# Fourteen weight-slice copies moved from VectorE to GpSimd, and five instead of eight plain-float32 tiles, in a fused attention and two-layer MLP kernel

## The chip, the cores and the metric

The kernel runs on one NeuronCore of a Trainium2 chip. The metric is the device time of one execution in microseconds. Engines are called as in the profile: PE is TensorE (matmul), PEld its weight loads, DVE is VectorE, ACT is ScalarE, POOL is GpSimd, SP issues the DMAs. A line number such as L405 is a line of the kernel before.

## The reference

Inputs are float32 (the weights arrive as 64-bit floats and are taken apart inside the kernel). First a linear recurrence per head over 768 steps, 4 batches, 8 heads, head size 48:

```
for t in range(S):
    cur   = u * k_t (outer) v_t
    y_t   = r_t @ (state + cur)
    state = w * state + k_t (outer) v_t
x = y, as 3072 rows of 384
h = x @ w_in              # 384 -> 2048, layer 1
g = h * tanh(softplus(h))
x = g @ w_out             # 2048 -> 384
h = relu(x @ w2_in)       # layer 2
out = (h * h) @ w2_out
```

## The kernel before, in words

The sequence is cut into 6 chunks of 128 steps. For each chunk the attention gives 512 columns of x (4 batches by 128 steps). `BLOCKS` lists 12 blocks of work, each one layer on one chunk; a block has 16 tiles, one for each slice of 128 of the 2048 hidden columns. Tile number i runs over all 192 tiles; tiles 0 to 15 are the first block, layer 1 on chunk 0. For each tile PE does an "up" product into a PSUM tile h (128x512), ACT and DVE apply the activation, and PE does a "down" product that is added into accumulators acc.

**Precision.** A float32 operand is written as the sum of a high part rounded to the shorter format fp32r and a low part (the rest, also fp32r). A product of two such pairs takes three fp32r matmuls (`mm3`, L809 to L812: high by high, high by low, low by high). So an up takes 9 matmuls, and a down of layer 1 too (3 column groups by 3). For tiles in the set `FULL` (L40) the down is done differently: `act1` does not split the activation g, and `down1` multiplies the unsplit g with the unsplit weight `WF[1, j]` in plain float32, 3 matmuls (L934), each of which the trace shows as two records. A tile in `FULL` therefore skips two DVE instructions in `halves`: the high part (L904) and the low part (L909). The product with h that comes before (L872) is done for both kinds.

**Weights.** `convert(layer, j, ...)` (L351 to L411) brings one slice of weights, 128x768, from 64-bit words to the pair of high and low part. For layer 1 the steps are: a DMA load `raw`; ACT L366 and L372; DVE L376 and L383, after which `f` (the ring "wf") is the float32 weight; the high part, `hi`; and on DVE L410 the low part, f minus hi. For slices 0 and 1 the high part is made by ACT (L407); for the other 14 (`j >= WHIGH`) by DVE (L405). The up of tile j in the first block needs hi and lo of slice j. The ring "wf" has 6 buffers, so slice j can't write f before the last reader of slice j-6 is done: the low part L410, or for a tile in `FULL` its plain-float32 down. Converted slices are stored to DRAM (`keep`) and loaded again for later blocks.

**Order.** The program is not written in the order in which it runs. Every step is given to `plan.add` with an engine, an assumed duration, a due time, and the tiles it reads and writes. `Plan.order` (L139) then plays a list schedule: at each moment each free engine takes, of the steps that are ready, the one with the earliest due time. The order that comes out is the order in which each engine's instructions are issued, and each engine works strictly in that order. A changed engine or duration of one step can so change the order of the others. Attention work for later chunks (`unit`) is spread among the tiles in the same way. The ScalarE functions of the first 32 tiles are done in groups (`GROUPS`): Tanh for each tile, then Arctan and Sin for a group, with a table load between.

POOL has very little work in this kernel: some memsets and four small copies (`pads`, L658), all in the first 14 us.

Of the kernel before, what the change touches and what calls it, by code (L numbers as in the profile page):

```python
# [36 lines left out]
TRIG = sum(GROUPS)  # L37
GROUP_OF = [(sum(GROUPS[:g]), n) for g, n in enumerate(GROUPS) for _ in range(n)]
HIGH, WHIGH = 32, 2
FULL = frozenset(range(0, 8))  # L40


class Tl:
# [67 lines left out]
class Plan:  # L111
# [8 lines left out]
    def add(self, eng, dur, due, fn, r=(), w=(), deps=(), late=0.0, table=""):  # L120

        it = dict(n=len(self.items), eng=eng, dur=dur, due=due, fn=fn, deps=list(deps), after=[], ready=0.0, late=late, table=table)
        for t in r:
            if t.writer:
                it["deps"].append(t.writer)
        for t in w:
            it["deps"] += t.readers
            if t.writer:
                it["deps"].append(t.writer)
        for t in r:  # L130
            t.readers.append(it)
            t.users.append(it)
        for t in w:
            t.writer, t.readers = it, []
            t.users.append(it)
        self.items.append(it)
        return it
# [67 lines left out]
def rwkv_moe_kernel(ctx: ExitStack, tc: tile.TileContext, good, rk, nat, wuT, wrow, ub, cst, w1, w2, out):  # L205
    nc = tc.nc
# [41 lines left out]
    def f32v(ap):  # L248
        return ap.bitcast(F32)
# [3 lines left out]
    add = plan.add  # L253

    def dma(o, i, eng=nc.sync):
        eng.dma_start(out=o, in_=i)
# [88 lines left out]
    def parts(layer, j, again=""):  # L345

        t = R[f"w{j}"].new([128, 2, 768], F32R, f"w{layer}_{j}{again}")
        W[layer, j] = [t.part(lambda ap, i=i: ap[:, i]) for i in range(2)]
        return t, *W[layer, j]

    def convert(layer, j, due, load_due):  # L351

        raw = R[f"w{j}"].new([128, 768, 2], U32, f"raw{layer}_{j}")
        t, hi, lo = parts(layer, j)
        f = WF[layer, j] = R["wf"].new([128, 768], F32, f"wf{layer}_{j}")
        src = (w1, w2)[layer - 1][j]

        def load():
            o = raw.get().rearrange("p (h d) t -> p h (d t)", h=2)
            dma(o, src.rearrange("h p d -> p h d").bitcast(U32))  # L360

        def fu():
            return f.get().bitcast(U32)

        def s0():
            nc.scalar.activation(f.get(), raw.get()[:, :, 1].bitcast(F32), AF.Copy, scale=HSC)  # L366

        on_act = layer == 1

        def s1():  # L370
            x = raw.get().rearrange("p d t -> p (d t)").bitcast(U8).rearrange("p (d t) -> p d t", t=8)[:, :, 3]
            nc.scalar.activation(raw.get()[:, :, 0].bitcast(I32), x, AF.Copy, scale=1 / 32, bias=-15.5 / 32)  # L372

        def s2():
            if on_act:
                nc.vector.scalar_tensor_tensor(  # L376
                    fu(), fu(), 3, raw.get()[:, :, 0], ALU.logical_shift_left, ALU.bitwise_or
                )
            else:
                nc.vector.tensor_scalar(fu(), fu(), 3, None, ALU.logical_shift_left)  # L380

        def s3():
            nc.vector.scalar_tensor_tensor(fu(), raw.get()[:, :, 1], 0x80000000, fu(), ALU.bitwise_and, ALU.bitwise_or)  # L383

        def s4():
            nc.vector.scalar_tensor_tensor(
                fu(), raw.get()[:, :, 0], 29, fu(), ALU.logical_shift_right, ALU.bitwise_or
            )

        it = add("SP", 0.786, load_due, load, w=[raw])  # L390
        if layer == 2:
            gates.append((it, int(load_due)))
        elif j >= 6:
            gates.append((it, -1))
        add("ACT", 0.9, due - 1.5, s0, r=[raw], w=[f])
        if on_act:
            add("ACT", 0.9, due - 1.3, s1, r=[raw], w=[raw])
            add("DVE", 0.96, due - 1, s2, r=[raw, f], w=[f])
            add("DVE", 0.96, due - 0.8, s3, r=[raw, f], w=[f])
        else:  # L400
            add("DVE", 0.55, due - 1, s2, r=[f], w=[f])
            add("DVE", 0.96, due - 0.8, s3, r=[raw, f], w=[f])
            add("DVE", 0.96, due - 0.6, s4, r=[raw, f], w=[f])
        if layer == 1 and j >= WHIGH:
            add("DVE", 0.56, due, lambda: nc.vector.tensor_copy(hi.get(), f.get()), r=[f], w=[hi])  # L405
        else:
            add("ACT", 0.87, due, lambda: nc.scalar.activation(hi.get(), f.get(), AF.Copy), r=[f], w=[hi])  # L407
        add(
            "DVE", 0.96, due + 0.5,
            lambda: nc.vector.tensor_tensor(lo.get(), f.get(), f32v(hi.get()), ALU.subtract), r=[f, hi], w=[lo],  # L410
        )  # L411
# [404 lines left out]
    def turn(i, extra=0.0):  # L816

        b = GROUP_OF[i][0] if i < TRIG else i
        return b + 0.02 * (i - b) + extra
# [18 lines left out]
    def act1(i, blk, h):  # L838

        e = R["e"].new([128, 512], F32, f"e{i}")  # L840
        full = i in FULL
        g = R["ghi"].new([128, 512], F32, f"g{i}") if full else e
        d = i + 1
        if i < TRIG:
# [6 lines left out]
            if i + 1 == sum(GROUP_OF[i]):  # L851
# [17 lines left out]
                for n, x, o, p in now:  # L869
# [3 lines left out]
                    )  # L873
                    late.append((n, o, None) if n in FULL else (n, *halves(n, o, turn(n, 2.2))))
            return late
# [21 lines left out]
    def halves(i, g, due, square=None):  # L897
        hi = R["ghi"].new([128, 512], F32R, f"ghi{i}")
        lo = R["glo"].new([128, 512], F32R, f"glo{i}")
        if square:  # L900
            add("ACT", 0.63, due, lambda: nc.scalar.activation(hi.get(), square.ap, AF.Square), r=[square], w=[hi])  # L901
        else:
            if i < HIGH:
                add("DVE", 0.42, due, lambda: nc.vector.tensor_copy(hi.get(), g.ap), r=[g], w=[hi])  # L904
            else:
                add("ACT", 0.63, due, lambda: nc.scalar.activation(hi.get(), g.ap, AF.Copy), r=[g], w=[hi])  # L906
        add(
            "DVE", 0.69, due + 0.2,
            lambda: nc.vector.tensor_tensor(lo.get(), g.ap, f32v(hi.ap), ALU.subtract), r=[g, hi], w=[lo],  # L909
        )  # L910
        return hi, lo
# [89 lines left out]
    for j in range(NF):  # L1001
        convert(1, j, j - 1, -140 + j)
# [21 lines left out]
    for i in range(NS):  # L1024
# [22 lines left out]
        if blk == 0:  # L1047
            keep(1, j, NF + j)
        elif blk + 1 < len(BLOCKS) and BLOCKS[blk + 1][0] != layer:
            if layer == 2:  # L1050
                again(1, j, i + LAG + 1)
            elif (2, j) in kept:
                again(2, j, i + LAG + 1)
            else:
                convert(2, j, i + LAG + 4 + 0.3 * j, i + LAG)
                keep(2, j, i + LAG + 14)
# [258 lines left out]
```

## Time and profile before

| | |
|---|---|
| runs (us) | 913.98, 917.95, 919.26; median 917.95 |
| profiled execution (us) | 914.35 |
| its span (us) | 912.6 |
| PE busy | 900.1 us (99%), 5225 instructions |
| DVE busy | 549.9 us (60%) |
| ACT busy | 581.1 us (64%) |
| POOL busy | 2.9 us (0%), 13 instructions |
| granted TensorE clock, mean | 0.997 of 2.4 GHz |

The span is the time from the first to the last instruction in the profile; the profiled execution's own time is 1.75 us longer. PE is the engine that is nearly always busy, so the questions to a change are how much PE work it takes away or adds, and where PE waits. Shares over the whole span hide that DVE is full in the first 110 us and much less so later.

### The profile page before, as it was taken

What the parts mean: (1) busy time and instruction counts of PE and PEld (TensorE: products, weight loads), DVE (VectorE), ACT (ScalarE), POOL (GpSimd) and SP (SyncE); (2) the same over time, 40 slices, a digit from 0 to 9 for tenths busy, and PEclk for the clock granted to TensorE, in tenths of its full rate; (3) what the DMA queues carried; (4) which work ended last, traced back from release to release, by engine and by line L of the source; (5) the groups of instructions that cost most, each with busy time, mean ns of one, the idle gap of its engine ahead of it and who ended that gap; (6) DMA issues with size and microseconds to landing.
All of it is one profiled execution on the core that took longest, in us unless ns stands there. A gap on an engine that the chain in (4) does not pass through costs nothing.

```text
span 912.6 us, 13415 instructions
## 1 busy us (share of the span) xinstructions
PE 900.1 (99%) x5225; PEld 755.1 (83%) x5225; DVE 549.9 (60%) x913; ACT 581.1 (64%) x1056; POOL 2.9 (0%) x13
## 2 busy tenths in 40 slices
PE   8999999999999999999999999999999999999997
PEld 6666888889888988788888888888888888899996
DVE  8999947999344448778885333224677876211212
ACT  6979768886445557777775454554677866544442
POOL 1000000000000000000000000000000000000000
PEclk9999999999999999999999999999999999999999
DMA  9995317995126664012665110655300355200001
GB/s 306 355 358 231 152 66 228 365 396 206 54 97 219 209 194 142 1 56 92 204 212 185 47 55 30 197 203 187 101 9 1 103 194 187 70 1 1 35 0 39
DMA packets 34537, 132.09 MB, mean 145 GB/s; under 512 B 3905, under 2 KB 8258, under 8 KB 34466
## 3 DMA queue, kind: packets, MB, share of 16 engines
q1 hardware_dynamic: 34466, 131.15, 42.0%
q8 instruction: 43, 0.70, 0.3%
q14 instruction: 28, 0.23, 0.1%
HBM read 100.27 MB, written 29.88 MB: 143 GB/s over the span
## 4 chain that ended last, share of the span: by engine, by line
PE 94%; DMA 4%; DVE 1%; SPq 0%; issue 0%; DVEq 0%
PE h L810 14%; PE h L812 14%; PE h L811 14%; PE acc L971 8%; PE acc L973 7%; PE acc L972 7%; PE acc L810 7%; PE acc L812 7%; PE acc L811 7%; DMA nat<-in_nat_dram 3%; PE sc L536 2%; PE y L606 2%; PE acc L934 2%; PE y L583 1%; DMA raw<-in_w_dram 1%; PE y L639 1%
## 5 line engine op out<-in xcount | busy, mean ns | idle before, releaser
L909 DVE TENSOR_TENSOR glo<-g,ghi 128x512 fp32r<-128x512 f32 x96 | 66.3, 691 | 218.7 <-ACT ghi L901 215.2
L917 ACT ACTIVATE e<-h 128x512 f32<-128x512 f32 x96 | 57.4, 598 | 175.1 <-PE h L812 175.0
L901 ACT ACTIVATE ghi<-e 128x512 fp32r<-128x512 f32 x96 | 59.7, 622 | 19.8 <-PE acc L972 19.8
L909 DVE TENSOR_TENSOR glo<-e,ghi 128x512 fp32r<-128x512 f32 x88 | 59.4, 687 | 17.2 <-ACT ghi L906 14.7
L887 ACT ACTIVATE e<-h 128x512 f32<-128x512 f32 x64 | 38.0, 594 | 39.4 <-PE h L812 39.2
L918 ACT ACTIVATE g<-e 128x512 f32<-128x512 f32 x96 | 60.7, 632 | 2.9
L892 DVE TENSOR_TENSOR e<-e,r 128x512 f32<-128x512 f32 x64 | 44.1, 689 | 26.2 <-ACT r L891 25.9
L509 ACT ACTIVATE A<-cst_sb,dg 128x128 f32<-128x128 f32 x168 | 52.9, 393 | 2.6 <-DVE dg L477 2.6
L906 ACT ACTIVATE ghi<-e 128x512 fp32r<-128x512 f32 x64 | 40.1, 627 | 17.4 <-DVE e L885 17.2
L890 ACT ACTIVATE r<-e 128x512 f32<-128x512 f32 x64 | 40.1, 627 | 13.9 <-DVE e L879 13.9
L882 DVE SCALAR_TENSOR_TENSOR r<-e,r 128x512 f32<-128x512 f32 x64 | 44.2, 690 | 1.7
L885 DVE SCALAR_TENSOR_TENSOR e<-r,h 128x512 f32<-128x512 f32 x64 | 43.8, 685 | 1.7
L971 PE MATMUL acc<-w,ghi 128*128 128x384 f32 x128 | 44.2, 345 | 0.0
L973 PE MATMUL acc<-w,glo 128*128 128x384 f32 x128 | 43.2, 337 | 0.0
L972 PE MATMUL acc<-w,ghi 128*128 128x384 f32 x128 | 43.1, 337 | 0.0
L888 ACT ACTIVATE e<-e 128x512 f32<-128x512 f32 x64 | 40.4, 632 | 1.7
L545 DVE COPY_PREDICATED A<-cst_sb,sc 128x512 f32<-128x512 int32 x48 | 33.8, 730 | 12.7 <-PE sc L536 12.7
L891 ACT ACTIVATE r<-r 128x512 f32<-128x512 f32 x64 | 40.3, 630 | 1.4
L810 PE MATMUL h<-xh_a,w 128*128 128x512 f32 x96 | 39.9, 416 | 0.0
L811 PE MATMUL h<-xl_a,w 128*128 128x512 f32 x96 | 37.6, 392 | 1.3 <-DVE xl_a L689 1.3
L457 DVE TENSOR_TENSOR rk<-rk,E 112x1024 f32<-112x1024 f32 x24 | 29.3, 1222 | 15.5 <-DMA rk<-in_rk_dram 15.4
L810 PE MATMUL h<-xh_b,w 128*128 128x512 f32 x96 | 37.7, 393 | 0.0
(486 smaller groups left out, 2489.0 us busy)
## 6 DMA issues: line engine op xcount, KB each, us to landing
raw<-in_w_dram SPq DMA_DIRECT2D x32, 768.0 KB, 9.9
wd<-w SPq DMA_DIRECT2D x32, 768.0 KB, 8.3
nat<-in_nat_dram SPq DMA_DIRECT2D x20, 576.0 KB, 5.1
rk<-in_rk_dram SPq DMA_DIRECT2D x24, 448.0 KB, 5.1
out_dram<-o SPq DMA_DIRECT2D x24, 192.0 KB, 1.9
w_0r<-wd SPq DMA_DIRECT2D x4, 768.0 KB, 4.3
w_1r<-wd SPq DMA_DIRECT2D x4, 768.0 KB, 5.7
w_2r<-wd SPq DMA_DIRECT2D x4, 768.0 KB, 5.5
```

Source lines behind the costliest of these rows:

```text
L509: nc.scalar.activation(a[:, p, :], anti, AF.Copy, scale=u["dg"][:, h:h + 1])
L810: nc.tensor.matmul(o, wh, xh, start=first, stop=False, skip_group_check=True)
L811: nc.tensor.matmul(o, wh, xl, start=False, stop=False, skip_group_check=True)
L812: nc.tensor.matmul(o, wl, xh, start=False, stop=last, skip_group_check=True)
L882: nc.vector.scalar_tensor_tensor(r.ap, e.ap, 2.0, r.ap, ALU.subtract, ALU.mult)
L901: add("ACT", 0.63, due, lambda: nc.scalar.activation(hi.get(), square.ap, AF.Square), r=[square], w=[hi])
L909: lambda: nc.vector.tensor_tensor(lo.get(), g.ap, f32v(hi.ap), ALU.subtract), r=[g, hi], w=[lo],
L917: add("ACT", 0.59, d, lambda: nc.scalar.activation(e.get(), h.ap, AF.Relu), r=[h], w=[e])
L918: add("ACT", 0.63, d + 0.2, lambda: nc.scalar.activation(g.get(), e.ap, AF.Square), r=[e], w=[g])
L971: nc.tensor.matmul(o, hi[:, sl], h_, start=(j == 0), stop=False, skip_group_check=True)
L972: nc.tensor.matmul(o, hi[:, sl], l_, start=False, stop=False, skip_group_check=True)
L973: nc.tensor.matmul(o, lo[:, sl], h_, start=False, stop=(j == NF - 1), skip_group_check=True)
```

## The change

The high part of the 14 layer-1 slices is issued on POOL instead of DVE, with an assumed duration of 0.9 us instead of 0.56 us in the plan. The set `FULL` shrinks from tiles 0 to 7 to tiles 0 to 4; tiles 5, 6 and 7 are split and use three fp32r matmuls as the tiles after them do.

```diff
@@ -37,7 +37,7 @@
 TRIG = sum(GROUPS)
 GROUP_OF = [(sum(GROUPS[:g]), n) for g, n in enumerate(GROUPS) for _ in range(n)]
 HIGH, WHIGH = 32, 2
-FULL = frozenset(range(0, 8))
+FULL = frozenset(range(0, 5))
 
 
 class Tl:
@@ -402,7 +402,7 @@
             add("DVE", 0.96, due - 0.8, s3, r=[raw, f], w=[f])
             add("DVE", 0.96, due - 0.6, s4, r=[raw, f], w=[f])
         if layer == 1 and j >= WHIGH:
-            add("DVE", 0.56, due, lambda: nc.vector.tensor_copy(hi.get(), f.get()), r=[f], w=[hi])
+            add("POOL", 0.9, due, lambda: nc.gpsimd.tensor_copy(hi.get(), f.get()), r=[f], w=[hi])
         else:
             add("ACT", 0.87, due, lambda: nc.scalar.activation(hi.get(), f.get(), AF.Copy), r=[f], w=[hi])
         add(
```

## Rows read from the trace of the kernel before

**Rows 1.** Busy time of each engine in stretches; the answer's columns stand in its first line.
```profile
core 0: us, PE busy (x) PEld busy (x) DVE busy (x) ACT busy (x) POOL busy (x), PEclk, DMA share, GB/s
28.00:112.00 84.00, 81.05 (x555) 56.22 (x554) 83.21 (x136) 70.89 (x113) 0.00 (x0) 1.00 0.72 263
112.00:912.60 800.60, 794.58 (x4448) 680.52 (x4446) 442.72 (x727) 491.85 (x904) 0.00 (x0) 1.00 0.37 126
```

**Rows 2.** Waits of PE, whole span: line, awaited; us in total, times, longest.
```profile
PE y L593 <- DVE A L545: 2.0, 1, 2.0
PE acc L934 <- DVE g L872: 1.7, 2, 1.5
PE h L811 <- DVE xl_a L689: 1.3, 1, 1.3
```

**Rows 3.** Chain that ended last, in order of time: start us, us, what.
```profile
28.26 13.83 DMA nat<-in_nat_dram
42.18 0.56 DVE nat L488
...
49.12 0.43 DVE w L405
...
50.43 0.61 DVE g L872
51.08 2.84 PE acc L934 x6
...
72.55 2.77 PE acc L934 x6
...
79.44 2.58 PE acc L934 x6
...
84.07 2.77 PE acc L934 x6
```

**Rows 4.** Timeline of PE, two split downs, then three ups: start us, us, engine, line, operation.
```profile
102.61 0.40 PE L810 MATMUL acc<-ghi,w 128*128 128x512 f32 x1
...
106.73 0.40 PE L810 MATMUL h<-xh_a,w 128*128 128x512 f32 x1
...
112.91 0.40 PE L810 MATMUL acc<-ghi,w 128*128 128x512 f32 x1
```

**Rows 5.** Groups on DVE, 28 to 112 us: count, busy us, mean ns, idle before.
```profile
L410 DVE TENSOR_TENSOR w<-wf,w 128x768 fp32r<-128x768 f32 x15 | 14.2, 950 | 0.0
L383 DVE SCALAR_TENSOR_TENSOR wf<-raw,wf 128x768 uint32<-128x768 uint32 x14 | 13.3, 950 | 0.0
L376 DVE SCALAR_TENSOR_TENSOR wf<-wf,raw 128x768 uint32<-128x768 uint32 x14 | 13.3, 949 | 0.0
L405 DVE CAST w<-wf 128x768 fp32r<-128x768 f32 x14 | 7.7, 551 | 0.0
L545 DVE COPY_PREDICATED A<-cst_sb,sc 128x512 f32<-128x512 int32 x8 | 5.6, 728 | 0.0
L872 DVE TENSOR_TENSOR g<-e,h 128x512 f32<-128x512 f32 x8 | 5.2, 679 | 0.0
```

**Rows 6.** Timeline of DVE: a weight copy, then a split of one tile, and what follows.
```profile
31.93 0.55 DVE L405 CAST w<-wf 128x768 fp32r<-128x768 f32 x1
32.39 0.95 DVE L376 SCALAR_TENSOR_TENSOR wf<-wf,raw 128x768 uint32<-128x768 uint32 x1
...
89.11 0.42 DVE L904 CAST ghi<-e 128x512 fp32r<-128x512 f32 x1
89.44 1.29 DVE L909 TENSOR_TENSOR glo<-e,ghi 128x512 fp32r<-128x512 f32 x2
90.64 0.69 DVE L515 TENSOR_TENSOR A<-cst_sb,dg 128x512 f32<-128x512 f32 x1
```

**Rows 7.** Timeline of POOL, whole span (part).
```profile
0.25 0.10 POOL L1298 MEMSET const-float32-0.0<- 128x1 f32 x1 [0.25 <-issue]
...
6.58 1.38 POOL L650 MEMSET pads<- 128x1536 f32 x1 [5.60 <-PE tps L331]
...
9.01 0.27 POOL L658 COPY pads<-nat 128x96 f32<-128x96 f32 x1 [0.72 <-DMA nat<-in_nat_dram]
```

**Rows 8.** Timeline of DVE, 9 to 15 us: one instruction beside the POOL copy, one later.
```profile
9.08 1.27 DVE L457 TENSOR_TENSOR rk<-rk,E 112x1024 f32<-112x1024 f32 x1
...
11.98 1.21 DVE L457 TENSOR_TENSOR rk<-rk,E 112x1024 f32<-112x1024 f32 x1
```

**Rows 9.** Timelines of DVE and PE: low parts of slices 2, 4, and their ups.
```profile
34.60 0.95 DVE L410 TENSOR_TENSOR w<-wf,w 128x768 fp32r<-128x768 f32 x1
...
36.22 0.50 PE L810 MATMUL h<-xh_a,w 128*128 128x512 f32 x1
...
40.48 0.95 DVE L410 TENSOR_TENSOR w<-wf,w 128x768 fp32r<-128x768 f32 x1
...
47.26 0.50 PE L810 MATMUL h<-xh_a,w 128*128 128x512 f32 x1
```

## The prediction

> **What bounds the kernel now.** I read three views in this order: busy time by stretch, the waits of PE, and the chain that ended last. The stretches [rows 1] show PE busy for 794.58 of 800.60 us after 112 us, so behind that point nothing but PE work can shorten the kernel. Both edits act before it: from 28 to 112 us, where layer 1's weights are converted, DVE is busy 83.21 of 84.00 us and PE 81.05. The reader is to see that both engines are full here: DVE has no room, yet PE hardly waits for it. The waits of PE [rows 2] say how little: 1.7 us for the plain-float32 downs (two waits, the longest 1.5) and 1.3 for a low part of x at 29 us. The third, 2.0 us for a masked copy, lies at 21 to 23 us, ahead of the first weight copy on DVE at 31.93 us [rows 6]; the two edits touch neither it nor the 1.3. The chain [rows 3] names what stands behind the 1.5 us wait: a load of nat, issued at 28.26 us, that lands at 42.18 us and starts a run of DVE work up to the activation product at 50.43 us, for which PE waits until 51.08 us. One weight copy (49.12 us, 0.43) stands in that run.
>
> So a gain can come from two places only: PE work that goes, and a part of that 1.7 us. A loss has no such cap, as DVE is full.
>
> **The change part by part.** The sum is made against the profiled execution, 914.35 us with a span of 912.6. The median shown, 917.95, is 3.6 us above it, and I add these 3.6 at the end.
>
> *Tiles 5, 6, 7 leave plain float32.* Their downs take 2.77, 2.58 and 2.77 us on the chain [rows 3], 8.12 together. A split down takes nine fp32r matmuls: two of them in a row run from 102.61 to 106.73 us, where the next up begins, or 2.06 us each [rows 4]. So PE loses 8.12 - 3 x 2.06 = 1.9 us of work. A change of operand kind costs PE some 0.1 us at a seam, which the chain's numbers already hold in part; I take 1.8. PE was not waiting at these places, so this comes off the time at once, if the split tiles' operands are there.
>
> Their cost: DVE gets three high parts and three low parts of the activation more. From start to start these take 0.33 us (89.11 to 89.44) and 0.60 (1.20 for two) [rows 6], so 3 x 0.93 = 2.8 us. It comes at 75 to 90 us, behind most of the relief below. It makes each of the three downs ready about 1 us later on its own chain, plus queueing; PE has ups of other tiles to go on with: from 106.73 to 112.91 us three of them stand in a row, 27 matmuls [rows 4]. I cost it at nothing on PE; without that cover it costs up to 2.8.
>
> The wf buffers of slices 5, 6 and 7 come free after the low part and no longer after the down. Slices 11 to 13 may start sooner; PE waits for none of them now, so nothing is gained.
>
> *Fourteen high parts go to POOL.* DVE loses 14 of the casts, 7.7 us of busy time [rows 5]; start to start one takes 0.46 us [rows 6], so 14 x 0.46 = 6.4 us of DVE's stream. Net of the splits DVE is relieved by 3.6 us. What that brings PE: the run behind the nat landing loses its one cast, so the 1.5 us wait shrinks by about 0.45. The three casts before 42 us (the one of rows 6 is the first) would only let DVE wait longer for the load. So 0.5 us, at most the 1.7 of the row, at least nothing.
>
> POOL's own time for 128x768 is in no row. Bounds from the nearest: a 128x1536 memset takes 1.38 us and a 128x1 one 0.10, so 0.83 ns for each column, and 0.10 + 768 x 0.83 ns = 0.74 us; a 128x96 copy takes 0.27, so (0.27 - 0.10) / 96 = 1.8 ns, and 1.46 us by that [rows 7]. The copy with the memset's slope gives 0.27 + 672 x 0.83 ns = 0.83. I take 0.85, an estimate, as most of the small copy must be fixed cost; POOL has nothing else to do then, so it is the time of one slice, not a queue. The high part comes some 0.3 us later than DVE's, with one more handover in and one back. The low part on DVE (L410) waits for it, and behind L410 stands everything of DVE. How much room is there? The tightest slice is 2: its low part starts at 34.60 us and takes 0.95, and its up at 36.22 follows 0.7 us after. The widest is 4: low part from 40.48, up at 47.26, 5.8 us after [rows 9]; the other slices lie between. Other DVE work stands between most copies and their low parts. I cost the longer handover at nothing, with an upper bound of 14 x (0.85 - 0.46) = 5.5 us if DVE stood still through all of them, and 14 x (1.46 - 0.46) = 14 with the long copy.
>
> *Do the two engines get in each other's way?* The trace has one place to look. A POOL copy runs at 9.01 to 9.28 us [rows 7], and the DVE product of two SBUF operands that begins at 9.08 takes 1.27 us, against 1.21 for the same instruction later [rows 8]. It is 0.06 us longer beside a copy that takes 0.27. It is one pair and small; it tells of some slowing, not of a stop of the copy's length.
> The Trainium skill, "SBUF — State Buffer", section "Who interferes with whom", speaks against the change: a VectorE instruction with two SBUF inputs and a GpSimd instruction that reads SBUF exclude each other, and the later one waits for the whole of the earlier. By that rule the instruction at 9.08 should have lost about 0.2 us, and the trace shows 0.06; whether a copy eight times as long does the same is not shown.
> My value: by the row, 0.06 / 0.27 = a fifth of the copy's time, 14 x 0.85 x 0.22 = 2.6 us of DVE; the relief of 3.6 still covers that. The upper end is priced as a rival.
>
> *Sum.* -1.8 (PE work) - 0.5 (wait) = -2.3 us: 914.35 - 2.3 = 912.05 for a profiled execution, with a span near 910.3, and 917.95 - 2.3 = 915.7 for the median.
>
> **The rivals.**
>
> *A, slower: the copies stop DVE.* Each copy takes DVE's second operand path for its whole length. In 28 to 112 us the six largest DVE groups [rows 5] hold 40.8 us of instructions with two SBUF operands (L410, L383, L376) and 10.8 with one operand in PSUM (L545, L872); the attention products, all smaller, are mostly of the first kind. Four copies in five would so meet one. Cost: 14 x 0.85 x 0.8 = 9.5 us against 6.4 saved, so +3.1, and the splits' 2.8 on top: DVE 5.9 us later at 112 us. DVE is full, so PE gets its last slices later by that; 1 to 2 us of room at the slices (0.7 at the tightest) go against it, and PE's saved work brings nothing where it waits. It comes to about +4.5 us, 922.5; with the copy at 1.46 us, 14 x 1.46 x 0.8 = 16.4 and some +11. It decides once a copy holds DVE for more than (6.4 - 2.8) / 14 = 0.26 us on average. For: DVE has 0.8 us idle in 84 [rows 1]. Against: the 0.06 us of rows 8. Chance 0.27.
> This is where the skill's rule above would lead.
>
> *B, more gain: the new order removes the waits.* With fourteen steps off DVE the plan is made anew; if the whole 1.7 us goes, and the 1.3 at 29 us with it, the sum is -1.8 - 3.0 = -4.8, 913. For: DVE is the releaser in both rows. Against: the first hangs on a DMA landing, the second comes before any moved copy. Chance 0.15.
>
> *C, nothing: the relief is used up.* The high part comes late by the upper copy time at the tight slices, and two or three waits of 0.6 to 0.9 us at L410 eat the 1.8 to 2.3 us: 917.5 to 918. That is also how it comes out if the new order brings as many small seams on PE as it removes. Chance 0.18.
>
> **How the numbers follow.** My forecast has 0.40, B 0.15, C 0.18, A 0.27. 0.5% is 4.6 us, about what a measurement of this kernel can tell from no change (the three runs themselves lie 5.3 us apart). Faster by more than that: half of B and a little of the forecast through the spread of runs, 0.14. Slower by more: just over half of A, with its long-copy end, and a little of C, 0.20. Within: 0.66. The range: the lower end takes in most of B and the runs' spread, 912.3; the upper reaches A at its likely price, 922.5. Without A the forecast's own range is 913 to 918.
>
> **What would show it.** Right: PE's busy time about 1.9 us down; 30 records of L934 instead of 48 (six for a tile [rows 3]); PE's wait for L872 at 1.2 us or less; 14 POOL copies of 0.7 to 1.0 us; DVE idle by some us in 28 to 112; the lines L410, L383 and L376 at 0.95 us as before. Wrong: these three lines with means well over 1 us or DVE idle ahead of L410 with POOL as the releaser (A, C), and new PE waits for weights between 36 and 110 us. If PE's waits fall by 3 us, B.

## The result, and the profile after

The changed kernel takes 921.81 us in the median of 9 runs, the kernel before 915.34 in 9 runs beside it. The ratio is 1.0059, 95% interval 1.0037 to 1.0080: some 5.4 us slower. The forecast was 2.3 us faster. Rival A (the copies stop DVE) has the sign and nearly the size, +4.5.

The profiled run has a span of 923.9 us, 11.3 above that of before. Not all of this is the change. The first up product of the first block starts at 34.17 us in it, against 27.92 before, and PE's instructions ahead of it are the same ones in the same order. What differs is TensorE's granted clock. The stretches of the kernel after (us, then busy us of each engine, PEclk the granted clock) show it:

```profile
core 0: us, PE busy (x) PEld busy (x) DVE busy (x) ACT busy (x) POOL busy (x), PEclk, DMA share, GB/s
0.00:10.80 10.80, 8.71 (x55) 5.30 (x55) 7.32 (x26) 3.03 (x7) 3.56 (x11) 1.00 0.82 219
10.80:24.50 13.70, 13.70 (x96) 11.88 (x96) 10.10 (x16) 8.29 (x24) 0.56 (x3) 0.50 1.03 380
24.50:35.00 10.50, 8.28 (x81) 6.49 (x77) 8.43 (x13) 8.00 (x12) 0.00 (x0) 0.84 1.04 398
35.00:99.50 64.50, 59.03 (x433) 40.61 (x434) 62.26 (x93) 54.74 (x88) 16.50 (x11) 1.00 0.74 261
99.50:103.00 3.50, 3.50 (x10) 2.75 (x9) 2.78 (x5) 1.81 (x5) 2.44 (x1) 0.51 0.00 0
103.00:120.00 17.00, 17.00 (x113) 13.51 (x112) 15.11 (x25) 12.85 (x20) 3.74 (x3) 1.00 0.32 119
```

PE ran at the lower level, 1.2 GHz, for 13.7 us near the start, and for 3.4 us more inside the next stretch, whose mean is therefore 0.84; in the profiled run of before that lasted 3.4 us in all (15.3 to 18.7). How long it lasts there differs from run to run (the mean granted clock of the nine runs of the change lies between 0.988 and 0.998), and the change isn't needed to set it: two of the variants below, one with the copies' place on POOL and one with five tiles, reach the first up at 27.65 and 27.84 us. So the start is set aside, and from here I also give the *inner time*: from the start of the first up to that of the up of tile 190, read from the timelines of PE. It is 861.7 us before and 866.5 after: 4.8 us lost behind the start. Where? The up of tile 2 starts at 41.89 us, 5.7 later than before [rows 9]; that of tile 14 at 116.57, 9.8 later [rows 4]. So 4.1 us go between tiles 2 and 14, another 1.0 near 190 us, and after that the distance stays the same to the end.

The waits of PE after, as in [rows 2]:

```profile
PE acc L811 <- DVE glo L909: 2.0, 1, 2.0
PE y L593 <- DVE A L545: 2.0, 1, 2.0
PE h L810 <- DVE e L872: 1.4, 2, 0.8
...
PE h L810 <- DVE g L872: 1.1, 1, 1.1
PE acc L934 <- DVE g L872: 1.0, 2, 0.9
...
PE h L811 <- DVE xl_a L689: 0.7, 1, 0.7
PE h L812 <- DVE w L410: 0.2, 1, 0.2
```

Behind the first up these are 6.4 us, against 3.0 before; the new ones are all for DVE. The longest ends at 98.36 us, and 1.2 us later the clock falls to half for 3.4 us: another 1.7 us. With gaps too short for this list counted too, PE's waits grew by 3.6 us; with the 1.7 that is 5.3, and the inner time grew by 4.8. So PE's own work fell by about 0.5 us only, where 1.9 was forecast; reckoned the same way, it fell by 1.4 in the run e4 below.

DVE from 28 to 118 us, as in [rows 5]:

```profile
L410 DVE TENSOR_TENSOR w<-wf,w 128x768 fp32r<-128x768 f32 x16 | 15.6, 978 | 3.5 <-POOL w L405 3.5
L383 DVE SCALAR_TENSOR_TENSOR wf<-raw,wf 128x768 uint32<-128x768 uint32 x15 | 14.8, 984 | 0.1
L376 DVE SCALAR_TENSOR_TENSOR wf<-wf,raw 128x768 uint32<-128x768 uint32 x15 | 14.2, 948 | 0.2 <-ACT raw L372 0.2
...
L488 DVE TENSOR_TENSOR nat<-nat,ub_sb 128x384 f32<-128x384 f32 x4 | 3.1, 769 | 0.0
```

The group L405 is gone from DVE. In its place DVE stands still for 3.5 us ahead of L410, for POOL, and the mean of L488 is 769 ns. Before, from 28 to 112 us, it was:

```profile
L488 DVE TENSOR_TENSOR nat<-nat,ub_sb 128x384 f32<-128x384 f32 x4 | 2.2, 552 | 0.8 <-DMA nat<-in_nat_dram 0.8
```

In all, seven DVE instructions behind 28 us take longer than the shortest of their kind, by 0.27 to 0.63 us, 3.4 us together, each beside a POOL copy; before, none does. POOL's timeline shows the other side:

```profile
9.63 1.19 POOL L658 COPY pads<-nat 128x96 f32<-128x96 f32 x1 [1.17 <-DMA nat<-in_nat_dram]
...
35.06 0.83 POOL L405 CAST w<-wf 128x768 fp32r<-128x768 f32 x1 [21.14 <-DVE wf L383]
40.43 2.31 POOL L405 CAST w<-wf 128x768 fp32r<-128x768 f32 x1 [4.54 <-ACT e L857]
...
97.82 4.12 POOL L405 CAST w<-wf 128x768 fp32r<-128x768 f32 x1 [4.76 <-DVE wf L383]
104.04 0.83 POOL L405 CAST w<-wf 128x768 fp32r<-128x768 f32 x1 [2.10 <-DVE wf L383]
```

A copy takes 0.83 us when nothing is in its way and up to 4.12. What DVE does in the 4.12:

```profile
97.63 1.28 DVE L909 TENSOR_TENSOR glo<-e,ghi 128x512 fp32r<-128x512 f32 x2
98.83 0.95 DVE L410 TENSOR_TENSOR w<-wf,w 128x768 fp32r<-128x768 f32 x1
99.70 0.68 DVE L515 TENSOR_TENSOR A<-cst_sb,dg 128x512 f32<-128x512 f32 x1
100.30 0.95 DVE L376 SCALAR_TENSOR_TENSOR wf<-wf,raw 128x768 uint32<-128x768 uint32 x1
101.97 0.96 DVE L410 TENSOR_TENSOR w<-wf,w 128x768 fp32r<-128x768 f32 x1 [0.72 <-POOL w L405]
102.85 0.95 DVE L383 SCALAR_TENSOR_TENSOR wf<-raw,wf 128x768 uint32<-128x768 uint32 x1
103.72 1.35 DVE L545 COPY_PREDICATED A<-cst_sb,sc 128x512 f32<-128x512 int32 x2
```

DVE runs five instructions with two SBUF operands one behind the other, and POOL does not get in. At 101.25 DVE has to stop for the very part that POOL is to make, and only then the copy runs: DVE stands 0.72 us, about one undisturbed copy. The next copy, at 104.04, falls beside L545, whose second source lies in PSUM, and takes 0.83. The Trainium skill, "SBUF — State Buffer", section "Who interferes with whom", has the pair exclusive for a whole instruction; these rows agree. That DVE can keep it over several instructions is this trace's.

Not every copy is kept out so long. This one got in behind a single instruction (L410), and the next, L488, was held:

```profile
47.68 1.44 POOL L405 CAST w<-wf 128x768 fp32r<-128x768 f32 x1 [0.93 <-DVE wf L383]
```

```profile
47.48 0.95 DVE L410 TENSOR_TENSOR w<-wf,w 128x768 fp32r<-128x768 f32 x1
48.35 1.17 DVE L488 TENSOR_TENSOR nat<-nat,ub_sb 128x384 f32<-128x384 f32 x1
```

The copy at 73.17 us does the same to L723. What decides between the two cases is not shown.

### The profile page after: what moved, and what is told of

It reads as the page before. It is cut to its first block, busy times and chain, and to the rows that moved or that the text cites. A ratio compares the mean times of both kernels' runs of the same rounds, so it can differ in the third digit from the quotient of the medians.

```text
span 923.9 us, 13465 instructions
## 1 busy us (share of the span) xinstructions
PE 907.0 (98%) x5234; PEld 762.8 (83%) x5234; DVE 550.7 (60%) x905; ACT 581.0 (63%) x1056; POOL 26.8 (3%) x27
## 4 chain that ended last, share of the span: by engine, by line
PE 88%; DVE 5%; DMA 3%; issue 1%; ACT 1%; POOL 1%; SPq 0%; POOLq 0%; DVEq 0%; ACTq 0%
PE h L810 14%; PE h L812 13%; PE h L811 13%; PE acc L971 8%; PE acc L973 7%; PE acc L972 7%; PE acc L810 6%; PE acc L812 6%; PE acc L811 6%; PE y L606 2%; PE sc L536 2%; DMA raw<-in_w_dram 2%; DMA nat<-in_nat_dram 2%; PE y L583 1%; DVE w L410 1%
## 5 line engine op out<-in xcount | busy, mean ns | idle before, releaser
L909 DVE TENSOR_TENSOR glo<-g,ghi 128x512 fp32r<-128x512 f32 x96 | 66.6, 693 | 215.4 <-ACT ghi L901 211.9
L917 ACT ACTIVATE e<-h 128x512 f32<-128x512 f32 x96 | 57.4, 598 | 175.1 <-PE h L812 175.1
L909 DVE TENSOR_TENSOR glo<-e,ghi 128x512 fp32r<-128x512 f32 x91 | 61.6, 689 | 16.8 <-ACT ghi L906 14.3
L906 ACT ACTIVATE ghi<-e 128x512 fp32r<-128x512 f32 x64 | 40.1, 627 | 18.7 <-DVE e L885 18.4
L890 ACT ACTIVATE r<-e 128x512 f32<-128x512 f32 x64 | 40.2, 627 | 15.3 <-DVE e L879 15.3
L545 DVE COPY_PREDICATED A<-cst_sb,sc 128x512 f32<-128x512 int32 x48 | 33.9, 733 | 13.8 <-PE sc L536 13.8
L810 PE MATMUL h<-xh_a,w 128*128 128x512 f32 x96 | 39.8, 414 | 1.7 <-DVE g L872 1.1
L810 PE MATMUL h<-xh_b,w 128*128 128x512 f32 x96 | 37.7, 393 | 0.8 <-DVE e L872 0.8
```

The costliest lines, as they stand in the source:

```text
L810: nc.tensor.matmul(o, wh, xh, start=first, stop=False, skip_group_check=True)
L917: add("ACT", 0.59, d, lambda: nc.scalar.activation(e.get(), h.ap, AF.Relu), r=[h], w=[e])
```

## The experiments

All of one group ran on one chip beside the kernel before. Inner time against that of before stands behind the ratio. It comes from one profile each. In the change, e1, e5, e7, e8, e9, e11 and e12 the first two tiles alone are 0.5 to 1.2 us faster than before, mostly because less is waited for just behind the first up, so their inner time reads too good by about that.

| run | copies | tiles in FULL | ratio to before, 95% interval | inner, us |
|---|---|---|---|---|
| the change | POOL | 5 | 1.0059 (1.0037 to 1.0080) | +4.8 |
| e1_pool_only | POOL | 8 | 1.0036 (1.0015 to 1.0058) | +2.2 |
| e2_five_only | DVE | 5 | 1.0051 (1.0027 to 1.0076) | +5.3 |
| e4_memset | POOL, no read | 5 | 0.9993 (0.9971 to 1.0014) | -0.3 |
| e8_memset_eight | POOL, no read | 8 | 0.9988 (0.9965 to 1.0012) | -1.3 |
| e5_extra | DVE, and POOL to spare | 8 | 1.0026 (1.0004 to 1.0047) | +1.8 |
| e3_old_order | POOL, order as for DVE | 5 | 1.0026 (1.0001 to 1.0052) | +3.2 |
| e6_act_five | ACT | 5 | 1.0025 (0.9998 to 1.0051) | +2.6 |
| e7_act_eight | ACT | 8 | 1.0014 (0.9988 to 1.0041) | +1.6 |
| e9_hold_five | DVE, buffers held | 5 | 1.0052 (1.0037 to 1.0067) | +3.8 |
| e10_hold_change | POOL, buffers held | 5 | 1.0148 (1.0125 to 1.0171) | +9.2 |
| e13_splits_off | DVE, no splits on DVE | 5 | 1.0023 (1.0001 to 1.0045) | +3.4 |
| e14_extra_splits | DVE, splits added | 8 | 1.0026 (1.0004 to 1.0048) | +4.1 |
| e11_act_late | DVE; ACT from slice 8 | 8 | 1.0000 (0.9981 to 1.0019) | +0.1 |
| e12_warm | DVE, more idle matmuls | 8 | 0.9991 (0.9975 to 1.0006) | -0.7 |
| e15_warm_act | DVE; ACT 8 to 11; as e12 | 8 | 0.9991 (0.9974 to 1.0008) | +0.8 |

A second measure uses every run and not one profile each: a run's span times its mean granted clock takes out, roughly, what the lower level cost PE (an estimate). Its mean is 909.2 to 909.5 us for the kernel before beside each of the four groups, 913.6 for the change, 912.6 for e1, 911.9 for e2, 909.0 for e4, 909.3 for e8, 912.1 for e5, 911.3 for e3, 911.5 for e13 and 912.6 for e14. The runs of one kernel scatter about these by 0.5 to 1.4 us (standard deviation).

**The two edits apart: e1 and e2.**

```diff
-            add("DVE", 0.56, due, lambda: nc.vector.tensor_copy(hi.get(), f.get()), r=[f], w=[hi])
+            add("POOL", 0.9, due, lambda: nc.gpsimd.tensor_copy(hi.get(), f.get()), r=[f], w=[hi])
```

> The copies on POOL alone, FULL stays at eight tiles. Theory 1 (a POOL copy and a DVE instruction with two SBUF operands shut each other out): 3 to 6 us slower than before, DVE waits ahead of L410 for POOL some 3 us in all, several two-operand instructions stretched by 0.3 to 0.6 us. Theory 2 (the remade order costs it): anything from -2 to +6, with the stretched instructions but PE waits elsewhere. Theory 3 (the three split tiles cost it): no slower than before, -0.5 to -1 us.

```diff
-FULL = frozenset(range(0, 8))
+FULL = frozenset(range(0, 5))
```

> FULL at five tiles alone, copies stay on DVE. Theory 1: -2 to 0 us against before (1.9 us of PE work goes, 2.8 us of DVE work comes into a full DVE). Theory 2: not told apart. Theory 3: 4 to 6 us slower, as the change is.

Each is slower alone, +3.3 and +4.7 us by the ratios; together they cost 5.4, less than the sum. e1 came out as theory 1 had it. e2 did not: theory 3, for which I had given little, is right about five tiles. The waits of PE in e2:

```profile
PE h L810 <- DVE e L872: 3.6, 3, 2.4
...
PE acc L934 <- DVE g L872: 2.0, 2, 1.5
```

and its stretches around the longest, which ends at 91.86 us:

```profile
28.00:92.80 64.80, 58.85 (x433) 40.85 (x433) 63.72 (x105) 57.27 (x92) 0.00 (x0) 1.00 0.81 294
92.80:96.20 3.40, 3.40 (x10) 2.62 (x9) 3.40 (x6) 0.87 (x2) 0.00 (x0) 0.50 0.00 0
96.20:112.00 15.80, 15.80 (x108) 12.83 (x108) 14.40 (x25) 8.84 (x15) 0.00 (x0) 1.00 0.19 64
```

An up waits for a PSUM buffer that the activation's product on DVE (L872) has still to read. DVE is late there, and again the clock is at half for 3.4 us just behind the wait.

**The sharing alone: e4, e8, e5.**

```diff
+            add("POOL", 0.9, due, lambda: nc.gpsimd.memset(hi.get().bitcast(F32), 0.5), r=[f], w=[hi])
```

> The changed kernel with each POOL copy replaced by a POOL memset of the same 128x768 tile: POOL writes and reads nothing, and the high parts are constants, which is part of the computation left out; the order on DVE and PE is that of the changed kernel. Theory 1: the loss goes, 2 to 4 us faster than before, two-operand instructions of DVE back at 0.95 us, no wait for POOL ahead of L410. Theory 2: stays 4 to 6 us slower than before. Theory 3: 3 to 5 slower.

> Copies as POOL memsets that read nothing (high parts constant: that part of the computation is left out), FULL at eight, order as in the run with the copies on POOL alone. It prices the relief of DVE without the sharing. Theory 1: 2 to 3 us faster than the run with POOL copies and FULL at eight, which is 0 to -1.5 us of before, with no stretched instruction on DVE. Rival (the remade order is what that run lost): as slow as that run, +2 to +3.

The memset waits for what the copy waited for (it writes where `raw` lies, so for L383), and DVE and PE have the order of the changed kernel to the instruction; only POOL's read is gone. The loss goes with it: 4.8 to -0.3 us inner, a ratio of 0.9993 where the change has 1.0059. POOL and DVE in e4, 27 to 112 us:

```profile
L405 POOL MEMSET w<- 128x768 f32 x14 | 10.4, 740 | 78.8 <-DVE wf L383 48.0 <-DMA raw<-in_w_dram 15.0 <-ACT e L847 4.7
...
L410 DVE TENSOR_TENSOR w<-wf,w 128x768 fp32r<-128x768 f32 x15 | 14.3, 955 | 0.0
L383 DVE SCALAR_TENSOR_TENSOR wf<-raw,wf 128x768 uint32<-128x768 uint32 x14 | 13.4, 955 | 0.0
```

All fourteen take 0.74 us whatever DVE does, no DVE instruction is stretched, none waits for POOL. That is theory 1 for the copies, and it clears the new order, and with it the longer handover. It also says how little there was to win: with the copies off DVE for nothing, eight tiles give -1.3 us and five -0.3, both within the interval of no change. I had expected -2 to -4 for e4; that part was too high.

```diff
+            add("POOL", 0.9, due, lambda: nc.gpsimd.tensor_copy(spare.get(), f.get()), r=[f], w=[spare])
```

> The kernel before, with fourteen POOL copies of the same float32 slices into a spare tile that nobody reads; the order on DVE and PE is that of before, so that only the sharing costs. Theory 1: DVE's two-operand instructions stretched by 3 to 5 us in all, time 1 to 4 us above before. Theory 2 and 3: no change, within 1 us.

+2.4 us by the ratio, with nobody waiting for the spare copies: the price of being stopped, without that of being late. One pair of its rows (POOL, then DVE; all its lines stand 2 or 3 further down) shows a cast on DVE, 0.55 us elsewhere, stopped by a POOL copy that got in first:

```profile
38.49 1.42 POOL L408 CAST spare<-wf 128x768 fp32r<-128x768 f32 x1 [0.94 <-DVE wf L385]
```

```profile
38.28 0.94 DVE L413 TENSOR_TENSOR w<-wf,w 128x768 fp32r<-128x768 f32 x1
39.15 1.18 DVE L407 CAST w<-wf 128x768 fp32r<-128x768 f32 x1
```

The copy waits through L413 (0.6 us), then runs its 0.83, and the cast ends 0.63 late. From the first up on, seven instructions of e5 are stretched so, by 0.17 to 0.65 us, 3.0 us in all (each against the shortest of its kind). Two of them are casts, with one SBUF operand: two-operand instructions are not the only ones that share with POOL's read.

**Is it the order? e3.**

```diff
-            add("DVE", 0.56, due, lambda: nc.vector.tensor_copy(hi.get(), f.get()), r=[f], w=[hi])
+            add("DVE", 0.56, due, lambda: nc.gpsimd.tensor_copy(hi.get(), f.get()), r=[f], w=[hi])
```

> Five tiles in FULL and copies issued on POOL, but the plan orders them as if they were DVE's, so that DVE and PE follow the order of the run with FULL at five alone, and each low part stands close behind its copy. Theory 1 (POOL's read and DVE's two-operand instructions shut each other out, and POOL gets in only where DVE stands still): DVE waits 0.72 us ahead of L410 for most of the fourteen, some 8 to 10 us against 6.4 saved, so as slow as five alone or slower, 4 to 9 us over before. Rival (the changed kernel's own order is the fault, not the sharing): clearly faster than the changed kernel, at most 2 us over before.

A miss of mine: +2.4 us, better than five alone and than the change, and DVE waits for POOL only twice, 1.4 us in all. With the same sharing the order decides how often DVE comes to a low part before its copy has got in. So the order matters too: the change is 3.0 us slower than e3 by the ratios, whose intervals overlap, 1.6 by the inner time and 2.3 by span times clock. It is not, as the rival had it, the whole.

**Another engine: e6, e7, e11.** The same line with `add("ACT", 0.87, ... nc.scalar.activation(hi.get(), f.get(), AF.Copy)`, for all fourteen slices or from slice 8.

> The changed kernel with the fourteen copies planned and issued on ACT (as for slices 0 and 1), FULL at five. Theory 1: no sharing, DVE relieved by 6.4 us; ACT gets some 11 us more into 13 free ones: between -2 and +2 us of before. Rival (five tiles are the fault whatever makes the copies): 4 us or more over before.

> The kernel before with the fourteen copies on ACT, FULL at eight. Theory 1: DVE relieved, nothing shared: -1.5 to +1 us of before, limited by the load of nat that the longest PE wait hangs on; ACT later at the activations may cost some of it.

> The kernel before with the copies of slices 8 to 15 on ACT and of 2 to 7 on DVE; FULL at eight. ACT has its idle time after 80 us and was what the early tiles waited for when all fourteen were on ACT: -1.5 to 0 us of before if DVE's relief counts there, +1 if ACT is late again at the activations near 120 us.

With the copies on ACT no DVE instruction is stretched, and ACT's copies take 0.83 to 0.88 us each; five tiles then cost +2.3 us (-0.2 to +4.7) instead of 5.4. With eight tiles nothing is gained either: in e7 PE waits for ACT at two score products (0.5 us each) and 0.8 us near 122 us for L872, and e11 has that last wait too (0.8 us), which eats the 1 us it was ahead at tile 14.

**Why do five tiles cost time? e9, e10, e13, e14.** Two ideas: the wf buffers that come free early let ACT convert slices 11 to 13 ahead of the activations (A), or the splits' work on a full DVE (B).

```diff
-        add("PE", 2.6 if full else 2.08, due, f, r=list(w) + [x for x in (hi, lo) if x], w=a)
+        add("PE", 2.6 if full else 2.08, due, f,
+            r=list(w) + [x for x in (hi, lo) if x] + ([WF[1, j]] if 5 <= i < 8 else []), w=a)
```

> FULL at five alone (copies on DVE), but the float32 slices 5 to 7 keep their wf buffers until their split downs are planned, as the plain-float32 downs made them do. Theory A (the buffers that come free early let ACT convert slices 11 to 13 ahead of the Arctan and Sin of the tiles that PE waits for): 2 us or more faster than five alone, its 2.4 us wait near 92 us gone. Theory B (the three splits, 2.8 us more on a full DVE, are it): as slow as five alone, 4 to 5.5 us over before, within 1 us.

> The changed kernel with the same hold of wf buffers 5 to 7. Theory A: 2 us or more faster than the change. Theory 1 (the sharing of POOL and DVE alone makes the change slow): within 1 us of the change, 4 to 6 us over before.

A falls: e9 is as slow as e2, though its wait at that place, near 93 us, is 1.5 us instead of 2.4. e10 is 13.5 us slower than before, which neither idea had; its longest wait of PE names the copy itself:

```profile
PE h L810 <- POOL w L405: 4.5, 1, 4.5
```

```profile
104.26 1.58 POOL L405 CAST w<-wf 128x768 fp32r<-128x768 f32 x1 [1.05 <-DVE wf L383]
```

```profile
104.21 0.94 DVE L410 TENSOR_TENSOR w<-wf,w 128x768 fp32r<-128x768 f32 x1
105.08 1.27 DVE L872 TENSOR_TENSOR e<-e,h 128x512 f32<-128x512 f32 x2
```

The copy is held through L410 and ends at 105.84, 0.76 us after DVE has begun L872, which reads h from PSUM. The hold made the last slices later, and PE waited 4.5 us for one of them.

```diff
+                add("DVE", 0.42, due, lambda: nc.gpsimd.memset(f32v(hi.get()), 0.5) if 5 <= i < 8 else nc.vector.tensor_copy(hi.get(), g.ap), r=[g], w=[hi])
...
+            lambda: nc.gpsimd.memset(f32v(lo.get()), 0.5) if 5 <= i < 8 else nc.vector.tensor_tensor(lo.get(), g.ap, f32v(hi.ap), ALU.subtract), r=[g, hi], w=[lo],
```

> FULL at five, copies on DVE, order of PE, ACT and DVE as in five alone, but the six split instructions of tiles 5 to 7 are POOL memsets that read nothing (these high and low parts are constants, so part of the computation is left out). Theory B (the splits' DVE work makes five alone slow): 3 us or more faster than five alone, -2 to +1.5 us of before, the 2.4 us wait near 92 us below 1. Rival (the order itself): stays at +4 to +5.

```diff
+    def gate(n, x, o, p):
+        nc.vector.tensor_tensor(o.get(), x.ap, p.ap, ALU.mult)
+        if 5 <= n < 8:
+            nc.vector.tensor_copy(spare[0], o.ap)
+            nc.vector.tensor_tensor(spare[1], o.ap, f32v(spare[0]), ALU.subtract)
```

> The kernel before, all else in its place, with a high-part copy and a subtraction into spare tiles on DVE for each of tiles 5 to 7 right behind their product: six instructions, 2.8 us of DVE, that nobody waits for. Theory B: +2 to +4 us, new PE waits for DVE between 80 and 112 us of some 2 to 3 us. Rival (order): within 1 us of before, as the up products have room.

e14 keeps everything of before in its place and adds the six instructions: +4.1 us inner, +2.4 by the ratio, +3.3 by span times clock, and the granted clock of its profile never falls behind the first up. There are two new waits of PE for DVE between 80 and 112 us (L840 is its L872, L917 its L909):

```profile
PE h L810 <- DVE e L840: 1.3, 2, 1.1
...
PE acc L811 <- DVE glo L917: 1.2, 1, 1.2
```

So 2.8 us put on DVE there come out at PE about one for one. e13 gives back 2.0 us inner and about half by the ratio (+2.1 us where e2 has +4.7, with intervals that overlap), but only 0.4 by span times clock. PE still waits 2.0 us at 89.80, but now DVE itself waits there, 1.0 us for the Sin on ACT, behind conversions that ACT does first. The splits have a price of their own, then (e14), and the order of the plan with five tiles has a share in e2; how the loss of e2 divides between them is not shown. Which step of that order it is, and what the 0.8 us near 190 us are that all runs with five tiles have, stays open.

**A faster version: e12, e15.** Four idle matmuls instead of two ahead of the first three score products (`busy(..., 4)`), in e15 with slices 8 to 11 on ACT.

> The kernel before with four instead of two idle matmuls ahead of each of the first three score products, 1.3 us of PE work more, in a stretch that ends in a wait of 2.0 us for DVE: order on DVE and ACT as before. If the granted clock then stays at its upper level from 5 to 35 us: 1 to 3 us faster in the median, as each 3.4 us at the lower level costs about 1.7. If it falls all the same: +0 to +1.3.

> The kernel before with four idle matmuls ahead of the first three score products and the copies of slices 8 to 11 on ACT. If the relief of DVE at 65 to 90 us counts and ACT has room for four: -1 to -2.5 us in the median; if ACT is late at the activations near 120 us as with eight of them: -0.5 to 0.

Neither beats the kernel before by what can be told. But the runs of e12 lie within 2.2 us (913.73 to 915.92) where those of before beside it lie within 6.1, and their mean granted clocks lie between 0.996 and 0.999 instead of 0.991 and 1.000: most of the spread goes with the clock, and it is gone with a busier PE near the start. The clock doesn't stay up altogether: the profile of e12 still has 3.4 us at the lower level, from 23.7 us.

## Why the prediction was wrong, point by point

Two steps of the prediction failed, and either alone is enough to turn its sign: the sharing of DVE and POOL, priced at 2.6 us of DVE that the relief would cover, and the splits on DVE, priced at nothing on PE. The copies alone (e1) came out 3.3 us slower instead of 0.5 faster, the five tiles alone (e2) 4.7 slower instead of 1.8 faster.

- **What bounds.** Right as far as it goes: both edits act before 112 us, and behind the last wait near 190 us the distance stays the same. What failed was the conclusion that a PE which hardly waits has room. DVE at 83.21 of 84.00 us [rows 1] was the row to weigh: the ups had work to go on with, but each wait for a PSUM buffer or a low part goes through DVE, and e14 shows what 2.8 us more cost there.
- **PE work, -1.8.** Too high. Its parts are right: L934 has 30 records, and split downs run at 2.06 us (in the change 2.08, from 103.94 to 106.02). But of PE's own work, waits and clock taken out, only 1.4 us went in e4 and 0.5 in the change, and that was paid for by waits.
- **"I cost it at nothing on PE", the splits.** Wrong. In e14 they cost 2.4 us by the ratio and 4.1 inner, about the 2.8 that I gave as the upper end or more, with no help from the clock. In e2 and the change the clock fell for 3.4 us behind a wait as well, another 1.7 us each, which no term held.
- **POOL's time for a slice, 0.85.** Right: 0.83 undisturbed.
- **"A fifth of the copy's time, 2.6 us of DVE".** The largest error: without POOL's read the loss is gone. In the change DVE loses 3.5 us in five waits ahead of L410 and 3.4 us in seven stretched instructions, 6.9 in all, more than the net relief of 3.6 and than the 6.4 of the casts themselves; e4 against the change prices it at 5.1 us inner. The reading of [rows 8] was at fault twice. The copy there started first and is mostly fixed cost, so the 0.06 us may be all of its reading, not a fifth of it. And I looked for what DVE loses, not for what POOL does: where DVE is first, the same small copy takes 1.19 us instead of 0.27 (9.63 us in the change), held by a DVE product that keeps its 1.22.
- **Handover at nothing.** Right by itself: from 27 to 112 us DVE never waits for POOL in e4, and twice in e8, 0.8 us in all. Wrong where the copy is held: five low parts were reached too early, 0.56 to 0.73 us each.
- **wf buffers free sooner, nothing gained.** e9 bears this out; holding them helps five tiles by nothing that can be told, and in the change it hurts.
- **The wait behind the nat load, -0.5.** It shrinks as forecast, to 0.9 us in the change and 0.5 in e4, from 1.5. But both have a new wait of 1.1 us near 50 to 57 us, of an up (L810) for the same product (L872), so nothing is gained.
- **The rivals.** A was the right one, with its threshold of 0.26 us a copy: DVE lost 0.49 on average (6.9 / 14). Its picture was half right: seven copies in fourteen stop a DVE instruction, ten are themselves held (1.18 us or more), and for five of these DVE pays at the low part. Its path to PE was another: PE waits 0.2 us for a slice; its other new waits are for activation products and split parts. That its +4.5 comes near the 5.4 is in part luck.

## What to carry to other kernels

Moving a copy to GpSimd frees VectorE only where VectorE's neighbours in time do not share its read; here those with two SBUF operands do, and in e5 a cast did. Beside a full stream of such instructions its time comes back, as stretched neighbours and as waits at the first reader, and in e5 it cost time though nobody waited for the copies. Where an engine is busy all through a stretch, price each microsecond added to it at about one, also if the bounding engine shows no wait for it yet. And split a two-part change before believing in it: here each part alone was slower.

## What the runs showed of the hardware

- A GpSimd cast of 128x768 from float32 to fp32r takes 0.83 us alone; VectorE's takes 0.55 [rows 6]. A GpSimd memset of that size takes 0.74 in e4, and no VectorE instruction beside it is stretched; one of the fourteen in e8 takes 0.91, beside a VectorE cast (91.25 us).
- VectorE instructions with two SBUF operands that follow one another kept a GpSimd copy waiting 3.3 us (97.82 us in the change), until VectorE stood still. A copy beside an instruction with a PSUM source took 0.83 (104.04 us). Copies at 47.68 and 73.17 us got in behind one two-operand instruction and held the next for 0.63 us.
- Between 85 and 110 us, at 2.4 GHz, each single wait of TensorE of 1.5 to 4.5 us was followed, within 1.2 us of its end, by 3.4 us at 1.2 GHz: in the change (wait of 2.0 us to 98.36, lower from 99.5 to 103.0), e2 (2.4 us to 91.86, lower from 92.8 to 96.2), e3, e9 (1.5 us), e10 and e13. That makes a wait of 2 us nearly twice as dear. Length alone does not decide: the 1.5 us wait at 51 us of before was not followed so, nor were waits of 2.0 to 2.7 us that end between 22 and 24 us (before, e2, e4, e14, e15), while in e5, e7 and e12 the clock did fall behind such a wait.
